# A planner's ranks, its DMA costs and a branch hint in a fused attention, experts and FFN kernel

## The chip, the cores and the metric

The kernel runs on one core of a Trainium2 chip. The metric is device time in microseconds, the median of repeated runs; lower is better. The engines are TensorE (PE, with its weight loads shown apart as PEld), VectorE (DVE), ScalarE (ACT), GpSimd (POOL) and SyncE (SP), which here only issues DMAs. Each engine takes its instructions strictly in the order in which they were written, and the engines wait for one another by semaphores.

## The reference

Three layers follow one another on 2 x 768 tokens: an attention in which a query sees only the keys of its own cluster, a layer of 8 experts of which each token takes one, and an FFN.

```python
# attention: q, k, v are [2, 8, 768, 64], 16 centroids for each head
q_assign = argmax(normed(q) @ normed(c).T)          # k_assign in the same way
scores = where(q_assign == k_assign, q @ k.T / 8, -1e9)
x = softmax(scores) @ v                             # -> [1536, 512]
# experts: w1 [8, 512, 1024], w2 [8, 1024, 512]
logits = x @ w_gate + modality_bias[modality_id]
e = argmax(logits);  p = softmax(logits)[e]
x = p * (relu(x @ w1[e]) @ w2[e])
# FFN: w_in [512, 2048], w_out [2048, 512], alpha [2048]
h = x @ w_in
out = (max(h, 0) + alpha * min(h, 0)) @ w_out
```

The weights of the FFN reach the kernel as 64-bit words. Most products are made from a high and a low part of each operand, in three matmuls.

## The kernel before

**Staging.** The attention runs over 8 groups, each one batch and two heads; a group has 12 units, each 128 queries of one head against all 768 keys. `group_prep` (line 710) prepares a group: it loads k, q and v (line 725), turns k and q on TensorE, finds clusters, moves halves of tiles between partitions (`move`), writes cluster masks (`mask_k`, `mask_q`) and makes fp16 parts of v (`v_abs` on ScalarE, line 916; `v_hi`; `v_lo` on VectorE, line 940). There is one buffer for raw v. `unit` (line 960) makes scores (line 973), the row maximum on VectorE (line 980), the exp on ScalarE (line 992), high and low fp16 parts, a DMA transpose of these (line 1026) into one of four buffers `pt`, and the product with v (line 1034). `group_out` stores the group's rows, and after a batch's last group `route` and `inverse` (lines 1140 and 1102) run chains of small VectorE operations that sort the tokens by expert, and matmuls of line 1134 that invert the order. `slot` (line 1338) is one tile of 128 tokens at one expert; there are 13. The first three use the weights as they are and fill gaps in the attention; the others split weights in two parts (ScalarE, then VectorE) and run after it, in buffers that the attention has left. Tiles that overflow the 13 slots are worked off in a branch (line 1685), which is skipped with these inputs. Ahead of it every engine reads three counts (line 1684).

**FFN.** Behind the branch, `ffn_weight` (line 1493) turns the 64-bit weights into fp32 parts in three VectorE steps (`wb1` to `wb3`, lines 1514 to 1519), then `wf_hi` and `wf_lo`; `gather` (line 1469) fetches the experts' rows in token order into `yg`, scales them (`gated`) and turns them; `ffn` (line 1526) runs, for each batch and each of 16 blocks of hidden columns, 24 first matmuls (line 1544), `neg` and `act` on VectorE (lines 1552 and 1555), `g_hi` on ScalarE, `g_lo` on POOL, and 18 second matmuls (line 1572) into six accumulators. Of eight banks of PSUM, two are left for the first matmuls; four buffers hold activations.

**What sets the order.** Nothing is issued as the code is written: each piece of work is an `Op` with a tag, its possible engines with a planned cost, and a rank `prio`. `Sched.run` (from line 207) plans them one by one on a simulated clock. On each engine, of the operations that could start within a margin `win` of the earliest, the one of lowest rank is taken; the engine for an operation is the one with the earliest planned end plus a `bias`. `ORDER` adds an offset to the rank of each kind (tag). For DMAs the planner keeps `dma_free`, the time up to which transfers are planned. A load of q, k, v or expert weights is kept back while much is planned:

```python
                if o.dma is not None and o.dma[1] == "load":
                    at = max(at, dma_free - self.back)
...
                xfer, kind, busy = o.dma[:3]
                way = "transpose" if kind == "transpose" else e
                dma_free = max(st + self.ISSUE[way], dma_free) + xfer
                o.end = dma_free + 0.13
                free[e] = st + 1.05 if e == "POOL" else max(st + busy, o.end - self.LEAD[way])
```

Then each engine's instructions are written in the planned order. All up to the branch is one plan; the FFN is another, with the same margins and an empty table of offsets (`TAIL`).

## Time and profile before

| | us |
|---|---|
| median of 3 runs | 755.58 (755.41 to 755.67) |
| the profiled execution | 757.23 |
| its span, first to last instruction | 755.4 |
| mean granted TensorE clock, 1 is full | 0.97 |
| TensorE busy | 689.2 |
| VectorE / ScalarE / POOL busy | 512.8 / 410.1 / 306.7 |

A profile is one execution. Times in its views count from the span's start. "Idle before" in a timeline stands in brackets, with what ended it; `ACTq` or `SPq` is an engine's own instruction queue (waits, branches, DMA issues), in which time is not counted as busy. The granted clock is the TensorE clock that the chip allowed, as a share of full speed. The DMA share is the mean busy share of the 16 DMA engines as the records give it, and can pass 1 a little.

### The profile page before, as it was taken

What the parts mean: (1) busy time and instruction counts of PE and PEld (TensorE: products, weight loads), DVE (VectorE), ACT (ScalarE), POOL (GpSimd) and SP (SyncE); (2) the same over time, 40 slices, a digit from 0 to 9 for tenths busy, and PEclk for the clock granted to TensorE, in tenths of its full rate; (3) what the DMA queues carried; (4) which work ended last, traced back from release to release, by engine and by line L of the source; (5) the groups of instructions that cost most, each with busy time, mean ns of one, the idle gap of its engine ahead of it and who ended that gap; (6) DMA issues with size and microseconds to landing.
All of it is one profiled execution on the core that took longest, in us unless ns stands there. A gap on an engine that the chain in (4) does not pass through costs nothing. (4 is left out here: it accounts for less than half of the span.)

```text
span 755.4 us, 13680 instructions
## 1 busy us (share of the span) xinstructions
PE 689.2 (91%) x5041; PEld 581.3 (77%) x5041; DVE 512.8 (68%) x913; ACT 410.1 (54%) x624; POOL 306.7 (41%) x276
## 2 busy tenths in 40 slices
PE   8878899786998779999898897899999999999997
PEld 7767787785777655568686786799999979999996
DVE  6798888889899741799897694587777533322331
ACT  5778988787889642388776894122222341111112
POOL 4467765573667432012232100365555622222221
PEclk9999999997999989999999899799999999999999
DMA  8498899799999989913755610234433030000002
GB/s 202 127 166 186 142 212 220 131 196 234 222 191 184 174 228 171 364 62 103 267 188 184 206 56 32 85 112 127 152 112 112 28 112 1 1 0 1 1 1 84
DMA packets 167418, 101.58 MB, mean 134 GB/s; under 512 B 133136, under 2 KB 147984, under 8 KB 167344
## 3 DMA queue, kind: packets, MB, share of 16 engines
q1 hardware_dynamic: 165136, 93.63, 51.1%
q0 software_dynamic: 2208, 7.00, 3.6%
q8 instruction: 42, 0.69, 0.4%
q14 instruction: 32, 0.26, 0.1%
HBM read 87.37 MB, written 12.85 MB: 133 GB/s over the span
## 5 line engine op out<-in xcount | busy, mean ns | idle before, releaser
L1572 PE MATMUL ps<-wf,ghl 128*128 128x512 f32 x576 | 140.1, 395 | 2.4 <-POOL ghl L420 1.5
L1572 PEld LDWEIGHTS ps<-wf,ghl 128*128 128x128 f32 x576 | 107.8, 189 | 25.2 <-POOL ghl L420 3.1
L1552 DVE TENSOR_SCALAR m<-ps,alp 128x384 f32<-128x384 f32 x64 | 39.5, 617 | 126.3 <-PE ps L1544 126.3
L392 ACT ACTIVATE ghl<-g 128x384 fp32r<-128x384 f32 x64 | 33.7, 526 | 166.7 <-DVE g L1555 166.7
L420 POOL TENSOR_TENSOR p<-p,p 128x768 f16<-128x768 f32 x57 | 95.7, 1682 | 46.1 <-ACT p L392 42.1
L420 POOL TENSOR_TENSOR ghl<-g,ghl 128x384 fp32r<-128x384 f32 x63 | 67.7, 1075 | 113.9 <-ACT ghl L392 113.9
L420 DVE TENSOR_TENSOR whl<-wst,whl 128x1024 fp32r<-128x1024 f32 x80 | 96.8, 1251 | 12.9 <-ACT whl L392 12.9
L980 DVE TENSOR_REDUCE nm<-pss 128x1 f32<-128x768 f32 x96 | 91.0, 950 | 12.3 <-PE pss L973 10.9
L992 ACT ACTIVATE p<-pss,nm 128x768 f32<-128x768 f32 x96 | 86.1, 899 | 22.1 <-DVE nm L986 7.0
L392 ACT ACTIVATE whl<-wst 128x1024 fp32r<-128x1024 f32 x80 | 82.3, 1057 | 11.3 <-PE ps L1458 6.9
L1034 PEld LDWEIGHTS <-pt 128*128 128x128 f16 x1152 | 60.9, 99 | 21.7 <-DMA pt<-p 12.9
L1034 PE MATMUL ps<-v,pt 128*128 128x65 f16 x1152 | 68.9, 196 | 9.2 <-DMA pt<-p 8.1
L1544 PE MATMUL ps<-x2a,wf 128*128 128x384 f32 x384 | 73.0, 347 | 4.0 <-ACTq L1685 4.0
L1544 PEld LDWEIGHTS ps<-x2a,wf 128*128 128x128 f32 x384 | 70.4, 195 | 5.7 <-ACTq L1685 4.4
L973 PE MATMUL pss<-s1k,s1q 128*128 128x384 f32 x192 | 60.1, 395 | 16.1 <-ACT p L992 15.4
L1544 PE MATMUL ps<-x2b,wf 128*128 128x384 f32 x384 | 69.8, 338 | 0.0
L1544 PEld LDWEIGHTS ps<-x2b,wf 128*128 128x128 f32 x384 | 67.7, 188 | 1.2
L1458 PE MATMUL ps<-whl,hTs 128*128 128x512 f32 x240 | 63.1, 401 | 2.0 <-DVE hTs L420 1.2
L1428 PE MATMUL ps<-whl,xTs 128*128 128x512 f32 x240 | 63.9, 407 | 1.0 <-ACT xTs L392 1.0
L420 POOL TENSOR_TENSOR wf<-tw,wf 128x1024 fp32r<-128x1024 f32 x16 | 40.5, 2532 | 55.8 <-ACT wf L392 55.8
L1458 PEld LDWEIGHTS ps<-whl,hTs 128*128 128x128 f32 x240 | 44.5, 190 | 13.1 <-DVE hTs L420 2.4
L1428 PEld LDWEIGHTS ps<-whl,xTs 128*128 128x128 f32 x240 | 45.3, 193 | 11.3 <-ACT xTs L392 1.4
(246 smaller groups left out, 1182.8 us busy)
## 6 DMA issues: line engine op xcount, KB each, us to landing
wst<-in_moe_w_dram SPq DMA_DIRECT2D x104, 512.0 KB
wst<-in_moe_w_in_dram SPq DMA_DIRECT2D x8, 1024.0 KB
wst<-in_moe_w_out_dram SPq DMA_DIRECT2D x8, 1024.0 KB
ys_d<-ys SPq DMA_DIRECT2D x13, 256.0 KB
raw<-in_k_dram SPq DMA_DIRECT2D x8, 384.0 KB
raw<-in_q_dram SPq DMA_DIRECT2D x8, 384.0 KB
vraw<-in_v_dram SPq DMA_DIRECT2D x8, 384.0 KB
x_d<-xg SPq DMA_DIRECT2D x8, 384.0 KB
```

The costliest lines, as they stand in the source:

```text
L392: nc.scalar.activation(out=out, in_=in_, func=AF.Copy)
L420: ENG[e].tensor_tensor(out=out, in0=a, in1=b, op=ALU.subtract)
L973: nc.tensor.matmul(s.t[:, jj, 0:HS], hd["12"[i], "q"].t[:, h, j, qs], hd["12"[i], "k"].t[:, h, jj], start=(i == 0), stop=(i == 1))
L980: S.op({"DVE": c_dve(SEQ)}, lambda e: nc.vector.tensor_reduce(out=nm.t, in_=s.t[:, :, 0:HS], axis=AX.XY, op=ALU.max, negate=True), r=[s], ...
L992: S.op({"ACT": c_act(SEQ) + 0.04}, lambda e: nc.scalar.activation(out=p.t, in_=s.t[:, :, 0:HS], func=AF.Exp, bias=nm.t), r=[s, nm], w=[p], ...
L1034: nc.tensor.matmul(o[:, c], pv, vv[:, D:VW], start=(i == 0), stop=(i == 2 * C - 1))
L1428: nc.tensor.matmul(hps[jj].t, lhs(xT, a, ci), rhs(ch, w_, cols), start=(ci == 0 and i == 0), stop=(ci == 3 and i == len(parts) - 1))
L1458: nc.tensor.matmul(yp.t, lhs(hT, a, f), rhs(4 + f // 2, w_, slice((f % 2) * 512, (f % 2 + 1) * 512)), start=(f == 0 and i == 0), stop=(f = ...
L1544: nc.tensor.matmul(hp.t[:, 0:HS], wi[:, a, kk, fs], x2b.t[:, bb, kk, sl], start=(n == 0), stop=(n == 3 * KD - 1))
L1552: S.op({"DVE": c_dve(HS) + 0.055}, lambda e: nc.vector.tensor_scalar(out=m.t, in0=hp.t[:, 0:HS], scalar1=0.0, scalar2=alp.t[:, f:f + 1], o ...
L1572: nc.tensor.matmul(view(), gh.t[:, a, tt * P:(tt + 1) * P], wo[:, bb, f % 2, :], start=(f == 0 and a == 0 and bb == 0), stop=(f == NF - 1 ...
```

## The change

No operation on data is added or taken away. The plan's inputs change, in six ways. `ORDER` has other offsets, for 43 kinds. `PULL` is new: a bias for an engine and a kind. The planned DMA costs change from a transfer time, an issue time and a lead to two times for each DMA (from issue to landing when the queue is empty, and from the landing before it) and a time for which a transpose holds the queue; `back` goes from 2.13 to 2.8, and only three expert slots (`FRESH`) are planned as loading new weights. Some planned costs and margins change. For the FFN, `TAIL` has offsets for five kinds, and there are margins and a `back` of its own. And the branch gets a label and a hint, marked ahead of all planned work, for PE, ACT and SP, that it is likely taken (which here is the jump past the overflow work).

```diff
-ORDER = {"chain_a": 5, "chain_g": 4, "chain_i": -20, "chain_r": -16, "chain_s": -43, "chain_v": -0.5, "consts3": 64,
-         "gate_exp": 29, "idle": 52, "logits": -46, "low": -0.5, "mm": 0.12, "mm2": 0.217, "move": 4, "nat_lo": 0.5,
-         "norm_ln": 71, "p_hi": -0.939, "pos_max": -17, "ptr": 1.658, "qk_hi": -0.534, "relu": 3, "row_max": 0.759,
-         "scaled": 1, "shift": -27, "sims_max": -45, "sm": 84, "smm": 2, "smtr": 1.5, "square_sum": 6, "tr": 78,
-         "tr_gather": 22, "v_hi": 1, "v_scale": -1, "w_lo": -0.161, "wb1": 0.5, "wb3": -7.5, "wf_lo": 46,
-         "xt_out": 3.5, "ys_out": 100, "ys_store": 56}
-
-TAIL = {}
+ORDER = {"avm": -1, "chain_h": 10, "chain_i": 8, "chain_r": -40, "chain_v": 2.02, "evac_hi": -83, "exp": 1,
+         "gated": -13, "late_consts6": 33, "lm": 8, "logits": -112, "mask_q": 56, "mm2": 0.079, "move": 14,
+         "norm_ln": 11, "onehot": -72, "otr": 1, "p_lo": -3.5, "place": 31, "ptr": 3.804, "qk_hi": 11, "relu": -19,
+         "row_max": 0.687, "scaled": -1, "shift": -35, "sims_eq": 1, "sims_max": 1, "sims_out": -31, "sm": 21,
+         "smm": 4, "smtr": -9, "square": 55, "tr": 18, "tr_gather": 93, "v_abs": 61, "v_hi": -48, "v_lo": -6,
+         "v_scale": -1.5, "v_turn": 1, "w_hi": -20, "wb2": 31, "wb3": 109, "ys_store": 37}
+
+PULL = {("gated", "POOL"): 2.1, ("qk_hi", "DVE"): 1.1, ("wf_hi", "ACT"): -2, ("ys_out", "ACT"): -1.1,
+        ("ys_out", "DVE"): -1}
+
+TAIL = {"mm_second": 69, "neg": 40, "tr_gather": 55, "wf_load": 72, "x2_hi": 103}
...
     LANDED = 0.05
-    ISSUE = {"transpose": 2.37, "SP": 1.86, "POOL": 1.9}
-    LEAD = {"transpose": 2.91, "SP": 5.8}
+    CHANGE = 0.3
+    HELD = {True: 1.1, False: 1.6, "load": 1.5, "store": 0.75, "transpose": 0.7}
...
         o.fn = fn
-        o.prio = (self.prio if prio is None else prio) + self.order.get(tag, 0.0)
+        o.prio = self.prio if prio is None else prio
+        o.prio += self.order.get(tag, 0.0)
         o.tag = tag
+        o.bias = {e: (self.bias if bias is None else bias).get(e, 0.0) + PULL.get((tag, e), 0.0) for e in o.eng}
         o.two = tag in TWO
...
         o.dma = dma
-        o.bias = self.bias if bias is None else bias
         o.adds = ()
...
         free = {}
-        dma_free = pool_till = dve_till = t0
+        dma_free = held = pool_dma = pool_till = dve_till = t0
+        last_kind = None
         ready = [o for o in ops if o.ndep == 0]
...
                     continue
-                if o.dma is not None and o.dma[1] == "load":
+                if o.dma is not None and o.dma[2] == "load":
                     at = max(at, dma_free - self.back)
...
                     if e == "DVE" and o.two:
-                        st = max(st, pool_till - 0.1)
-                    if e == "POOL" and not (o.dma and e in (o.dma[3:] or (e,))):
+                        st = max(st, pool_till + 0.01)
+                    if e == "POOL" and not (o.dma and e in (o.dma[4:] or (e,))):
                         st = max(st, dve_till)
+                        if o.tag == "move":
+                            st = max(st, pool_dma + 0.1, pool_till + 0.1)
                     cost = st + c + o.bias.get(e, 0.0)
...
             o.on = e
-            moved = o.dma is not None and e in (o.dma[3:] or (e,))
+            moved = o.dma is not None and e in (o.dma[4:] or (e,))
             if moved:
-                xfer, kind, busy = o.dma[:3]
-                way = "transpose" if kind == "transpose" else e
-                dma_free = max(st + self.ISSUE[way], dma_free) + xfer
-                o.end = dma_free + 0.13
-                free[e] = st + 1.05 if e == "POOL" else max(st + busy, o.end - self.LEAD[way])
+                first, later, kind, busy = o.dma[:4]
+                if kind == "transpose":
+                    done = max(st + busy, held)
+                    free[e] = done + 0.1
+                    first += done - st + (0.0 if last_kind == kind else self.CHANGE)
+                else:
+                    free[e] = st + busy
+                dma_free = max(st + first, dma_free + later)
+                o.end = dma_free
+                held = dma_free - self.HELD[kind]
+                last_kind = kind
+                if e == "POOL":
+                    pool_dma = dma_free
             else:
...
                     pool_till = free[e]
+                    if o.tag == "move":
+                        free[e] += 0.12
             ready.remove(o)
...
     BIG = float(2.0 ** 60)
-    N = dict(s1q=2, s1k=2, s2q=2, s2k=2, p=3, p16=5, pt=4, v16=2, wf_early=2, xs=2, whl=3, whl2=3, whi='A', wlo='D', lead=1, tw=1, wdma=1.0, pss=2, ps1=4, sq=1, bd=1.5, bp=0, ulead=4, pa=2, pb=0, nat=3, hi='*', lo='DP', lo0='PPT', vraw=1, mvp=1, mvb=0, epi=1, rM=2, lob=0.5, idle=40, pace=57, mve='PA', wd=0.3, wa=0.04, wp=0.03, wpl=0.03, wsp=0.07, cs=1, back=2.13, nld=8, lump='cs', mp=90, mps=8, mpn=0, trp=0.5, evp=3, xTs2=0, xtp=9, fl=6, rsh=1, rp0=0, go=-4, so=0, pre=0, fws=5, gs=4, eb=0.8)
+    N = dict(s1q=2, s1k=2, s2q=2, s2k=2, p=3, p16=5, pt=4, v16=2, wf_early=2, xs=2, whl=3, whl2=3, whi='A', wlo='D', lead=1, tw=1, pss=2, ps1=4, sq=1, bd=1.5, bp=0, ulead=4, pa=2, pb=0, nat=3, hi='*', lo='DP', lo0='PPT', vraw=1, mvp=1, mvb=0, epi=1, rM=2, lob=0.5, idle=40, pace=57, mve='PA', wd=0.3, wa=0.06, wp=0.03, wpl=0.04, wsp=0.04, cs=1, back=2.8, nld=8, lump='cs', mp=90, mps=8, mpn=0, trp=0.5, evp=3, xTs2=0, xtp=9, fl=6, rsh=1, rp0=0, go=-4, so=0, pre=0, fws=5, gs=4, eb=0.8)
+    FRESH = ((0, 2), (1, 1), (1, 5))
     W_EARLY = N["wf_early"]
...
                 t.t.rearrange("p h c d -> p h (c d)"),
-                src[b, hs].rearrange("h (p c) d -> p h (c d)", c=C)), w=[t], dma=(0.51, "load", 0.4),
+                src[b, hs].rearrange("h (p c) d -> p h (c d)", c=C)), w=[t], dma=(3.35, 1.5, "load", 0.55),
                 prio=S.prio + (6 if nm == "v" else 0), tag="load_qkv")
...
             n = G * HS
-            ways = {"SP": 0.65, "POOL": c_pts(n), "DVE": c_dve(n, True), "ACT": c_act(n)}
+            ways = {"SP": 0.65, "POOL": c_pts(n), "DVE": c_dve(n, True), "ACT": c_act(n) + 0.2}
             S.op({x: c for x, c in ways.items() if x[0] in N["mve"] + "S"}, fn,
-                 r=[(src, x) for x in K(sp_, sy)] + (zeros if z else []), w=[(dst, x) for x in K(part, y)], dma=(1.42, True, 0.6, "SP"), bias=mv_bias, tag="move")
+                 r=[(src, x) for x in K(sp_, sy)] + (zeros if z else []), w=[(dst, x) for x in K(part, y)], dma=(2.85, 0.95, True, 0.65, "SP"), bias=mv_bias, tag="move")
...
             S.op({"SP": 0.06}, lambda e: nc.sync.dma_start_transpose(out=p16t(pt), in_=p16.t.rearrange("p a s -> p (a s)")),
-                 r=[(p16, 0), (p16, 1)], w=[pt], dma=(1.91, "transpose", 1.43), tag="turn")
+                 r=[(p16, 0), (p16, 1)], w=[pt], dma=(2.7, 1.2, "transpose", 1.43), tag="turn")
         a = accumulator()
...
             S.op({"SP": 0.6 if c0 == 0 else 0.06}, load, r=[(ei, b), (fl, b)], w=[(wst, c0 + x) for x in range(nl)],
-                 dma=((3.44 if always else N["wdma"]) * nl / 2, "load", 0.38), prio=p0 - 5,
+                 dma=(*((3.75, 1.6) if always or (b, j) in FRESH else (0.0, 0.0)), "load", 0.39), prio=p0 - 5,
                  deps=[] if pace is None else [units[pace + c0]], tag="w_load")
...
             in_offset=bass.IndirectOffsetOnAxis(ap=inv.t[:, b, j:j + 1], axis=0)),
-            r=[(inv, b), *xd[0:b + 1]], w=[xs], dma=(0.9, False, 0), prio=p0 - 5, tag="rows_in")
+            r=[(inv, b), *xd[0:b + 1]], w=[xs], dma=(4.6, 1.2, False, 1.05), prio=p0 - 5, tag="rows_in")
         tp = S.new(ps_1)
...
         gather(t, x2[0], posc, NU + 4 + pslot * (MAIN[0] + N["gs"]) + t, own)
+    tc.mark_branch_hint_location("over", "LikelyTaken", [mybir.EngineType.PE, mybir.EngineType.Activation, mybir.EngineType.SP])
     order = S.run()
...
     S.order = TAIL
+    S.back = 12.4
+    S.win = {"DVE": 0.08, "ACT": 0.9, "PE": 0, "POOL": 0.44, "SP": 99}
...
     nb = [nc.values_load(nsl2.t[0:1, b:b + 1], min_val=0, max_val=SLOTS[1]) for b in range(B + 1)]
-    with tc.If(nb[B] > 0):
+    with tc.If(nb[B] > 0, label="over"):
         for b in range(B):
```

The DMA costs left out here change in the same way in every other call that issues a DMA.

## Rows read from the trace of the kernel before

**Rows 1.** Page of the profile, section 1: busy us (share of the span) xinstructions.

```profile
PE 689.2 (91%) x5041; PEld 581.3 (77%) x5041; DVE 512.8 (68%) x913; ACT 410.1 (54%) x624; POOL 306.7 (41%) x276
```

**Rows 2.** Busy time by stage: stretch (us), length, then busy us (xinstructions) of each engine, granted TensorE clock (1.00 is full), DMA share, GB/s.

```profile
160.00:265.00 105.00, 87.75 (x1004) 73.86 (x1000) 91.73 (x193) 84.40 (x128) 60.56 (x51) 0.92 1.11 203
265.00:282.00 17.00, 12.81 (x100) 8.49 (x100) 9.18 (x19) 7.91 (x12) 5.56 (x6) 0.80 0.79 230
282.00:302.00 20.00, 18.64 (x196) 10.33 (x193) 1.95 (x6) 4.81 (x7) 4.84 (x3) 1.00 1.03 172
302.00:468.00 166.00, 156.75 (x728) 118.33 (x726) 138.54 (x210) 121.55 (x162) 29.14 (x19) 0.98 0.46 165
468.00:488.00 20.00, 14.07 (x47) 11.78 (x48) 7.59 (x9) 3.24 (x5) 7.43 (x6) 0.74 0.31 95
...
595.00:626.00 31.00, 29.15 (x149) 24.57 (x148) 10.30 (x17) 11.44 (x20) 11.64 (x12) 1.00 0.26 85
```

**Rows 3.** Instructions of line 1685, the branch: duration ns min/median/max, first and last start us.

```profile
L1685 DVEq COMPARE_BRANCH  x1: 72/72/72, 465.2 to 465.2; - x1
L1685 DVEq EVENT_SEMAPHORE  x1: 21/21/21, 465.5 to 465.5; - x1
L1685 PEldq COMPARE_BRANCH  x1: 3619/3619/3619, 466.0 to 466.0; - x1
L1685 SPq COMPARE_BRANCH  x1: 58/58/58, 468.9 to 468.9; - x1
L1685 ACTq COMPARE_BRANCH  x1: 50/50/50, 469.1 to 469.1; - x1
...
L1685 ACTq EVENT_SEMAPHORE  x1: 17/17/17, 471.8 to 471.8; - x1
```

**Rows 4.** Timeline of TensorE, 440 to 510 us: start us, length us, line, idle before it, releaser.

```profile
462.84 5.05 PE L1458 MATMUL ps<-whl,hTs 128*128 128x512 f32 x21
471.87 6.89 PE L1544 MATMUL ps<-x2a,wf 128*128 128x384 f32 x24 [3.98 <-ACTq L1685]
...
479.76 1.89 PE L1572 MATMUL ps<-wf,ghl 128*128 128x512 f32 x7 [0.49 <-POOL ghl L420]
482.56 0.73 PE L1572 MATMUL ps<-wf,ghl 128*128 128x512 f32 x2 [0.92 <-ACT ghl L392]
...
499.83 4.39 PE L1544 MATMUL ps<-x2a,wf 128*128 128x384 f32 x24
```

**Rows 5.** Busy time in two stretches of 2 us at the branch (columns as in Rows 2).

```profile
470.00:472.00 2.00, 0.14 (x1) 0.14 (x1) 0.00 (x0) 0.00 (x0) 0.00 (x0) 0.60 0.10 30
472.00:474.00 2.00, 2.00 (x7) 2.00 (x8) 0.00 (x0) 0.00 (x0) 0.56 (x1) 0.50 0.03 8
```

**Rows 6.** Timeline of VectorE, 470 to 484 us.

```profile
478.88 1.90 DVE L1517 SCALAR_TENSOR_TENSOR tw<-wst,tw 128x1024 int32<-128x1024 int32 x1
480.71 0.60 DVE L1552 TENSOR_SCALAR m<-ps,alp 128x384 f32<-128x384 f32 x1
```

**Rows 7.** Timeline of SyncE's DMA queue, 222 to 302 us.

```profile
244.89 19.93 SPq L1026 DMA_TRANSPOSE pt<-p  x9
...
267.44 1.21 SPq L725 DMA_DIRECT2D vraw<-in_v_dram  x1
...
280.98 15.46 SPq L1026 DMA_TRANSPOSE pt<-p  x8
```

**Rows 8.** Timeline of VectorE, 216 to 221 us.

```profile
218.06 1.15 DVE L940 SCALAR_TENSOR_TENSOR v<-vraw,vsc,v 128x384 f16<-128x384 f32 x2 [0.68 <-ACT v L394]
```

**Rows 9.** Busy time of 2 us in the tail of the attention (columns as in Rows 2).

```profile
277.00:279.00 2.00, 2.00 (x7) 1.35 (x6) 1.15 (x2) 1.58 (x3) 0.84 (x1) 0.50 0.05 17
```

**Rows 10.** Timeline of TensorE around the routing of batch 0.

```profile
179.20 0.19 PE L1134 MATMUL ps<-T,M 128*128 128x6 f16 x2 [3.63 <-ACT xg L1057]
```

**Rows 11.** Timeline of TensorE, 244 to 249 us.

```profile
248.01 0.20 PE L1034 MATMUL ps<-v,pt 128*128 128x65 f16 x1 [3.11 <-DMA pt<-p]
```

**Rows 12.** Instructions on the tile yg, the rows gathered for the FFN.

```profile
L401 POOL TENSOR_SCALAR yg<-yg,gate x5: 692/697/1880, 393.5 to 611.3; 128x512 f32<-128x512 f32 x5
```

## The prediction

> **What bounds the kernel now.** I read the page's busy shares first, then the busy time cut by stage, then the places where a stage loses time. TensorE is busy 689.2 of 755.4 us and no other engine passes 513 [rows 1], so at most 66 us can come from its idle time, and something more from stretches in which its clock is low. The stage table [rows 2] shows where. From 160 to 265 us, the attention of batch 1, four things are nearly full at once: the DMA engines (share 1.11), VectorE (91.73 of 105), ScalarE (84.40) and TensorE (87.75, at a granted clock of 0.92); an order that helps one of them alone wins little. From 265 to 282 us TensorE does 12.81 of 17 us at clock 0.80, while VectorE and ScalarE are half idle: nothing is full there but, for most of it, the DMA engines. From 302 to 468 us, the experts, TensorE has 156.75 of 166: little is left. From 468 to 488 us, around the branch, it has 14.07 of 20 at clock 0.74. From 595 to 626 us, where batch 1 enters the FFN, 1.85 of 31 are idle; the rest of the FFN has none but its end. So the places that can pay are the end of the attention and the branch.

> **The branch hint.** The branch of line 1685 is skipped with these inputs. VectorE leaves it at once: its compare takes 72 ns and its next semaphore comes 0.3 us after [rows 3]. TensorE's own compare takes 3619 ns, begun at 466.0 while the last matmuls still run. ScalarE's takes 50 ns at 469.1, but its next instruction comes only at 471.8, and that is what releases TensorE: its last expert matmuls start at 462.84 for 5.05 us, and the first of the FFN starts at 471.87 after 3.98 us of idle time, released by ACTq L1685 [rows 3, 4]. So the wait that ends last is the 2.65 us on ScalarE behind a branch that itself takes 0.05. VectorE shows that such a wait need not be. The three engines that the change hints are the long branch and the two other late ones. If the jump's target is there in time, ScalarE is through at about 469.2, TensorE's own compare is long over, SP's is at 468.9, and the FFN starts 2.6 us earlier. Not removed: the reads of the count ahead of the branch.

> [...]

> Second, the clock. [...] Sum for the hint: 2.6 + 2.5 = 5.1 us.

> **The new plan's DMA costs, and one load.** In the planner a load of q, k, v or expert weights may not start before the DMA time planned so far less `back`. Before, SP is free again 2.78 us ahead of the end of a transpose's transfer (its end is 0.13 later, and 2.91 is taken off), and `back` is 2.13: a load comes 0.65 us after SP is free, so a transpose that is ready in that time goes first, whatever the load's rank. After, SP is free 2.6 us ahead of that end and `back` is 2.8: the load may start as soon as SP is free, and its rank (some 20 ahead of the transposes of its time) puts it first. The trace shows the loss. There is one buffer for raw v. VectorE's last use of it for group 6 starts at 218.06 and lasts 1.15 us [rows 8]; the load of group 7's v is issued at 267.44, after runs of transposes such as nine in 19.93 us [rows 7]: 48 us late. Without v the products of group 7 can't start, their four transposed buffers stay full, and the last eight transposes only start at 280.98; in the stage that holds this, TensorE idles 4.19 us, and at clock 0.80 loses as much as 0.20 x 17 = 3.4 more [rows 2]; the DMA engines, until then full, stand at 0.05 for two us [rows 9]. An early load lets the transposes run on; what is queued behind it on SP waits for its issue, 1.21 us. The gain is bounded from below by the DMA gap, which can be closed even if transposes are the limit (about 2 us), and from above by TensorE's whole loss, 7.6 us. I take 5, nearer the middle: the stage before is full of DMA work, so not all comes through, while what was waited for (12 tiles' products) also ends sooner and lets the experts' second weight buffers open earlier, a stage where VectorE is at 138.54 of 166.

> **The table of 43 kinds.** Most offsets reorder work on engines that are full between 160 and 265 us, where the sum of the work is unchanged; I count that at 0. One can be named. The routing chains of batch 0 had ranks -43 and -20 ahead of the row maxima and now have 0 and +8, behind them. Now TensorE stops there once for 3.63 us [rows 10]. In the whole stage the clock can cost as much as 0.08 x 105 = 8.4 us [rows 2]; I allow this stop a third, 2.8. So the bounds are 0 and about 6.5 us, and I take 0, because the DMA engines (1.11) set the end of that stage. The bias against gating on POOL moves up to five scalings of 0.697 us [rows 12] to engines that were not full in the FFN: 0. The other offsets have no row of their own; I bound them by one border between groups that stalls, 6 us (below), and the same gained. The plan's other new costs (transfers, reciprocals, moves on ScalarE, three expert slots marked as loading anew) change no instruction, only the order, and are in the same bound.

> **The FFN.** Ranking the second matmuls 69 back changes little: only two accumulator banks and four activation buffers let the first ones run ahead. It lets batch 1 start ahead of batch 0's last second matmuls; at most the 1.85 us of idle time at 595 to 626 [rows 2]. Against it, `neg` 40 back puts the weight steps ahead of it on VectorE. Now one such step of 1.90 us starts just before it and delays it to 480.71, and TensorE waits 0.49 and 0.92 us for what follows [rows 4, 6]. One more step ahead costs 1 to 2 us at the start; later two spare banks hide it. I take 0, bounds 2 us slower and 2 faster. The margins of 0.9 on ScalarE and 0.44 on POOL choose among waiting evictions of 31 us where these engines are a third busy [rows 2]: 0. SyncE's margin of 99 there puts output stores ahead of weight loads; the longer `back` of 12.4 touches no load of the FFN, as these aren't marked as held back: 0.

> **The sum.** 2.6 + 2.5 + 5 + 0 + 0 = 10.1 us. The profiled execution took 757.23 us with a span of 755.4; the median of the runs is 755.58. Taken off the execution this is 747.1, off the median 745.5, and I predict the median: 745.5.

> **Rivals.**
> - The hint does nothing, because the target is not held over 466 us: 755.6 - 5 = 750.6. [...] Against it: VectorE shows that a jump at this place can be through in 0.3 us; no row shows how long a hint holds, so its chance is a judgment.
> - The load comes early but the DMA engines set the end anyway, or other orders take the gain back: 755.6 - 5.1 = 750.5. For it: the share of 1.11.
> - More comes through: the routing stop goes too, 745.5 - 6.5 = 739.0. Against it: the same share.
> - Slower. The abs of v on ScalarE is now ranked 61 back. Without it the next group's products can't start, and ScalarE runs 84.40 of 105 us, so it may wait through a group's worth of exps, as it now waits for its load. A border that stalls like the one measured costs between 4.19 and 7.6 us, say 6, and a smaller one is in the trace already: 3.11 us of waiting for a transpose [rows 11]. The load's gain then goes as well. With one border the change breaks even, 755.6 - 5.1 + 6 = 756.5; from two on it is slower, 762.5. Against it: in each group ScalarE has a fifth of its time free, and a step of rank 61 back takes the first gap.

> **How the numbers follow.** Chances: forecast 0.45, hint without effect 0.13, load without gain 0.15, more 0.08, slower 0.19. A measurement can tell about 0.2%, 1.5 us. Of the two middle rivals about half a tenth ends within that of 755.6: same 0.07, faster 0.74, slower 0.19. The range reaches from the sum with all upper bounds but the FFN's (7.6 for 5, 6.5 for 0: 736) to a little past one stalled border, 758; only the cases beyond either end are left out.

> **What the changed profile would show.** Hint: the compare on TensorE well under 1 us, ScalarE's next instruction within 0.3 us of its compare, TensorE idle about 1.3 us before the FFN, the first 24 matmuls in about 4.4 us. Load: the eighth v load issued within some us of the last use of the buffer, no gap in the transposes before the last group's end, and the FFN's start earlier by about 5 us plus the hint's share. Wrong would be: ScalarE idle in front of the abs of v at several borders, or a longer stretch from 160 to 302 us; or TensorE idle after 488 us, which would put the fault into the FFN.

## The result and the profile after

The changed kernel takes **741.94 us** (median; 741.18 to 743.36) against 755.5 us for the kernel before: ratio 0.982 [0.981, 0.984], 13.6 us faster. 745.5 was predicted, in a range of 736 to 758. The profiled execution took 741.18 us, its span is 739.2 where that of before is 755.4. All line numbers are some 18 to 21 higher than before (the branch is line 1706).

The page of after, section 1, busy us and share of the span, answers to [rows 1]: TensorE is busy 10.5 us less for the same 5041 instructions, which is clock (0.986 on the mean instead of 0.97; in the three other runs of the changed kernel it is 0.974 to 0.980), and idle 60.5 instead of 66.2 us, 5.7 less.

```profile
PE 678.7 (92%) x5041; PEld 574.3 (78%) x5041; DVE 511.6 (69%) x916; ACT 410.1 (55%) x630; POOL 310.8 (42%) x274
```

Busy time by stage of after, with the columns of [rows 2]:

```profile
160.00:265.00 105.00, 87.35 (x986) 72.85 (x985) 85.79 (x187) 81.21 (x122) 60.88 (x58) 0.94 1.09 210
265.00:282.00 17.00, 12.94 (x178) 10.57 (x174) 11.46 (x19) 10.90 (x14) 6.56 (x5) 1.00 1.03 197
282.00:302.00 20.00, 18.27 (x174) 10.97 (x171) 4.87 (x11) 8.58 (x14) 6.19 (x4) 1.00 0.83 186
...
319.00:456.00 137.00, 133.96 (x645) 105.64 (x643) 126.61 (x143) 115.61 (x153) 30.05 (x16) 1.00 0.43 147
456.00:476.00 20.00, 17.52 (x82) 16.06 (x83) 11.02 (x14) 4.53 (x8) 8.40 (x7) 0.91 0.31 94
482.00:580.00 98.00, 95.08 (x473) 84.57 (x472) 71.46 (x82) 23.51 (x34) 55.82 (x35) 1.00 0.33 110
580.00:611.00 31.00, 30.64 (x157) 26.35 (x156) 10.15 (x17) 12.38 (x22) 10.10 (x9) 1.00 0.26 85
```

and the stage of before that answers to 319 to 456 us:

```profile
319.00:468.00 149.00, 139.75 (x654) 109.08 (x652) 127.00 (x147) 117.63 (x155) 28.14 (x18) 0.98 0.41 143
```

I split both spans at two points: the first split of an expert's weights on ScalarE (tile whl), and the end of the last expert matmul. Before: 319.3, then 148.6, then 287.5 us. After: 319.1, 136.4 and 283.8. So the attention, for which half of the gain was predicted, gave nothing; **12.2 of the 16.2 us come from the experts' stage**, of which the prediction said that little is left; and 3.7 lie from the branch on, of which up to 1.7 is a second stretch at half clock, from 484.1 to 487.5 us, that the trace of before alone shows there. Of the 12 us between the two stage rows, 6.2 are idle time of TensorE (9.25 to 3.04) and 5.8 busy time: 3.4 of these are clock, as will be seen, the rest some work that now lies ahead of the stage (x654 to x645).

The branch, as in [rows 3]: instructions of line 1706, duration in ns and start, and ahead of them the hint, which the trace has under line 1769 at 0.8 us (TensorE's at 0.9), some 450 us before the branch.

```profile
L1769 ACTq BRANCH_PREFETCH_HINT  x1: 45/45/45, 0.8 to 0.8; - x1
...
L1706 PEldq COMPARE_BRANCH  x1: 481/481/481, 453.8 to 453.8; - x1
...
L1706 ACTq COMPARE_BRANCH  x1: 68/68/68, 456.8 to 456.8; - x1
L1706 ACTq EVENT_SEMAPHORE  x1: 17/17/17, 457.2 to 457.2; - x1
```

TensorE's timeline of after around it, and further on in the FFN (start, length, idle before and its releaser), as in [rows 4]:

```profile
457.30 6.00 PE L1562 MATMUL ps<-x2a,wf 128*128 128x384 f32 x24 [1.84 <-ACTq L1706]
464.12 0.74 PE L1590 MATMUL ps<-wf,ghl 128*128 128x512 f32 x2 [0.82 <-ACT ghl L410]
...
495.62 4.49 PE L1562 MATMUL ps<-x2a,wf 128*128 128x384 f32 x24 [1.03 <-DVE g L1573]
```

ScalarE is through 0.4 us after its compare instead of 2.65, TensorE's compare takes 0.48 instead of 3.62 us, and the idle time is 1.84 instead of 3.98. But 24 matmuls still take 6.00 us and not 4.39. SyncE's queue, as in [rows 7]: the load of the last group's v is issued at 226.75, 40.7 us earlier, and the attention ends no sooner for it.

```profile
226.75 0.40 SPq L743 DMA_DIRECT2D vraw<-in_v_dram  x1
...
236.31 25.49 SPq L1044 DMA_TRANSPOSE pt<-p  x11
```

What the experts' stage lost before is a stop that stands in no row of the prediction. Three timelines of the kernel before, of POOL, ScalarE and TensorE:

```profile
408.72 0.96 POOL L1474 DMA_INDIRECT yg<-ys_d,posc  x1 [0.30 <-issue]
```
```profile
415.38 0.72 ACT L394 ACTIVATE yg<-yg,gate 128x512 f32<-128x512 f32 x1 [5.00 <-DMA yg<-ys_d,posc]
416.00 0.58 ACT L1437 ACTIVATE hb<-ps 128x512 f32<-128x512 f32 x1
```
```profile
416.63 1.12 PE L1451 MATMUL ps<-ident,hb 128*128 128x128 f32 x4 [4.23 <-ACT hb L1437]
```

POOL issues a gather of expert outputs for the FFN at 408.72. ScalarE stands in front of the scaling of these rows from 410.4 to 415.38, 6.7 us after the gather's issue; behind it in the same queue is the relu of the next expert (hb), and behind that TensorE. The planner before put the gather's landing at 1.9 + 0.9 + 0.13 = 2.93 us after its issue, the changed one at 3.9, where no other transfer is planned ahead of it. Behind the stop the clock is low too: from 415 to 422 us before, and in the same stretch after (columns of [rows 2]):

```profile
415.00:422.00 7.00, 5.37 (x15) 4.40 (x16) 4.18 (x4) 5.50 (x8) 0.00 (x0) 0.56 0.80 286
```
```profile
415.00:422.00 7.00, 7.00 (x34) 5.78 (x33) 4.92 (x6) 5.27 (x7) 0.00 (x0) 1.00 0.85 294
```

### The profile page after: what moved, and what is told of

It reads as the page before. It is cut to its first block, busy times and chain, and to the rows that moved or that the text cites. A ratio compares the mean times of both kernels' runs of the same rounds, so it can differ in the third digit from the quotient of the medians.

```text
span 739.2 us, 13709 instructions
## 1 busy us (share of the span) xinstructions
PE 678.7 (92%) x5041; PEld 574.3 (78%) x5041; DVE 511.6 (69%) x916; ACT 410.1 (55%) x630; POOL 310.8 (42%) x274
## 5 line engine op out<-in xcount | busy, mean ns | idle before, releaser
L1590 PE MATMUL ps<-wf,ghl 128*128 128x512 f32 x576 | 137.7, 392 | 1.5 <-ACT ghl L410 0.8
L1590 PEld LDWEIGHTS ps<-wf,ghl 128*128 128x128 f32 x576 | 107.1, 188 | 23.5 <-POOL ghl L438 1.6
L438 POOL TENSOR_TENSOR ghl<-g,ghl 128x384 fp32r<-128x384 f32 x62 | 70.6, 1142 | 122.0 <-ACT ghl L410 116.7
L438 DVE TENSOR_TENSOR whl<-wst,whl 128x1024 fp32r<-128x1024 f32 x80 | 93.7, 1215 | 3.5 <-ACT whl L410 3.4
L1052 PEld LDWEIGHTS <-pt 128*128 128x128 f16 x1152 | 60.5, 99 | 37.0 <-DMA pt<-p 31.2
L1562 PEld LDWEIGHTS ps<-x2a,wf 128*128 128x128 f32 x384 | 68.6, 192 | 8.4 <-DVE g L1573 4.9
L1573 DVE SCALAR_TENSOR_TENSOR g<-ps,m 128x384 f32<-128x384 f32 x64 | 35.6, 556 | 52.6 <-POOL ghl L438 50.4
```

The costliest lines, as they stand in the source:

```text
L438: ENG[e].tensor_tensor(out=out, in0=a, in1=b, op=ALU.subtract)
L1052: nc.tensor.matmul(o[:, c], pv, vv[:, D:VW], start=(i == 0), stop=(i == 2 * C - 1))
L1562: nc.tensor.matmul(hp.t[:, 0:HS], wi[:, a, kk, fs], x2b.t[:, bb, kk, sl], start=(n == 0), stop=(n == 3 * KD - 1))
L1573: S.op({"DVE": c_dve(HS)}, lambda e: nc.vector.scalar_tensor_tensor(out=g.t, in0=hp.t[:, 0:HS], scalar=0.0, in1=m.t, op0=ALU.max, op1=ALU. ...
L1590: nc.tensor.matmul(view(), gh.t[:, a, tt * P:(tt + 1) * P], wo[:, bb, f % 2, :], start=(f == 0 and a == 0 and bb == 0), stop=(f == NF - 1 ...
```

## The experiments

All in one table; the three columns in the middle are the stretches defined above, read from each kernel's trace. On the chips of these runs the kernel before spreads from 748 to 760 us, so times are compared as ratios to it, and the stretches tell where. Executions of one order differ too. Before, hint_only, gather_late and hint_gather run the same instructions in the same order up to the first split and reach it at 313.1 to 319.3 us (mean 315.3); the five kernels with the changed order (changed, run again, after_no_hint, after_old_ffn, after_gather) reach it at 317.9 to 320.1 (mean 319.0). So the new order of the attention gains nothing and may cost some 4 us.

| kernel | to the first split | experts | branch to end | median us | ratio to before |
|---|---|---|---|---|---|
| before | 319.3 | 148.6 | 287.5 | 755.5 | 1 |
| changed | 319.1 | 136.4 | 283.8 | 741.94 | 0.982 [0.981, 0.984] |
| changed, run again | 317.9 | 135.6 | 284.4 | 742.69 | 0.986 [0.982, 0.990] |
| hint_only | 314.0 | 148.9 | 282.5 | 749.80 | 0.994 [0.992, 0.997] |
| after_no_hint | 319.9 | 135.6 | 287.1 | 742.57 | 0.984 [0.979, 0.988] |
| gather_late | 313.1 | 141.0 | 284.3 | 743.61 | 0.988 [0.983, 0.993] |
| v_load_early | 326.5 | 132.6 | 286.6 | 747.75 | 0.992 [0.988, 0.995] |
| hint_gather | 314.6 | 140.8 | 281.2 | 739.72 | 0.982 [0.977, 0.986] |
| three | 325.5 | 135.2 | 280.4 | 745.21 | 0.988 [0.984, 0.992] |
| plan_only | 332.2 | 137.9 | 284.2 | 757.18 | 1.003 [1.000, 1.007] |
| order_only | 346.4 | 147.5 | 283.9 | 777.75 | 1.027 [1.022, 1.033] |
| routing | 335.4 | 134.1 | 285.7 | 757.81 | 1.003 [0.999, 1.007] |
| after_old_ffn | 320.1 | 135.5 | 281.8 | 737.43 | 0.977 [0.972, 0.981] |
| after_gather | 318.0 | 141.6 | 285.9 | 746.47 | 0.989 [0.985, 0.994] |

**The hint alone**, in the kernel before.

```diff
+    tc.mark_branch_hint_location("over", "LikelyTaken", [mybir.EngineType.PE, mybir.EngineType.Activation, mybir.EngineType.SP])
     order = S.run()
-    with tc.If(nb[B] > 0):
+    with tc.If(nb[B] > 0, label="over"):
```

> The kernel before, with the branch label and the hint and nothing else. If the hint acts by itself: TensorE's compare falls from 3.62 us to under 1, ScalarE's next instruction comes 0.3 to 0.5 us behind its compare instead of 2.65, and the FFN starts about 2.1 to 2.6 us earlier: 753.0 of 755.5. If the clock then stays up, as the prediction had it, 2.5 us more: 750.4; in the changed kernel the first 24 matmuls took 6.00 us, so I now expect only part of that. Rival: what shortened the idle time in the changed kernel is its new order ahead of the branch, and the hint does nothing: 755.5.

It gives 4.2 us [2.1, 6.3]. TensorE in the trace of hint_only:

```profile
464.70 6.00 PE L1544 MATMUL ps<-x2a,wf 128*128 128x384 f32 x24 [1.80 <-ACTq L1686]
```

The idle time falls by 2.2 us. The clock still falls behind it, for 3.4 us instead of 6.8: in the matmuls the gain is 0.9, not 2.5.

**The changed kernel without the hint**, the two lines above taken out.

> The changed kernel without the label and the hint. If the hint acts: idle time ahead of the FFN goes back to about 4 us, and the time is 2.1 to 4.5 us above the changed kernel's 741.9, so 744.0 to 746.5. Rival: no change, 741.9.

The idle time of 3.99 us is back in front of the FFN, and the last stretch is 287.1 us against 283.8 and 284.4: 3 us in the trace. The times don't resolve it: 742.57 us lies below the 744.0 to 746.5 expected.

**The gather planned later**, in the kernel before, so that its landing is planned 5.0 us behind its issue; nothing else (`dma_free` moves with it, and so do the transfers planned behind a gather).

```diff
-   ... w=[yg], dma=(0.9, False, 0), tag="rows")
+   ... w=[yg], dma=(3.0, False, 0), tag="rows")
```

> The kernel before, with one planned cost changed: the gather of the experts' rows is planned to land 5.0 us after its issue instead of 2.9 (its transfer is planned as 3.0 instead of 0.9). The order up to about 388 us stays as it was. Theory from the two traces: most of the gain lies in the experts' stage, and there in waits like the one of 4.23 us before 416.63, where ScalarE's scaling of a gathered row sat for 5.00 us in ScalarE's queue, planned too early, and held up the relu behind it; a later planned landing takes that wait and the low clock behind it (3.4 us of work) away: 748 to 750. Rival: the stage won by the table's offsets for the experts' evictions, and this cost alone gives nothing: 755.5.

9.1 us [5.7, 12.6] faster. The instructions keep their order up to 388 us, so what lies ahead of that (313.1 instead of 319.3) is the spread between executions, which hint_only shows with 314.0 as well. The experts' stretch is 141.0 against 148.6 and 148.9 with the stop: 7.6 to 7.9 us, as expected of a stop of 4.2 us and 6.8 us at half clock (4.2 + 3.4). In the trace of **hint_gather**, hint and gather together, ScalarE no longer scales these rows here, and the clock stays up. The wait itself is not gone. The gather issued at 402.76 is waited for until 411.30, longer than before, but by POOL, and neither ScalarE nor TensorE stands behind it:

```profile
402.76 1.97 POOL L1474 DMA_INDIRECT yg<-ys_d,posc  x1 [0.30 <-ACT x2a L392]
...
411.30 1.17 POOL L401 TENSOR_SCALAR yg<-yg,gate 128x512 f32<-128x512 f32 x1 [5.69 <-DMA yg<-ys_d,posc]
```
```profile
415.00:422.00 7.00, 7.00 (x34) 5.77 (x34) 7.00 (x8) 6.40 (x10) 1.52 (x2) 1.00 0.86 328
```

> The kernel before with the hint and the later planned gather landing, nothing else. If the two gains are of different places, they add: 0.9944 and 0.9879 of before give 0.9823, the same as the whole change. Rival: the later gather's 9 us held some of the hint's (both runs had shorter low clock at the FFN's start), and the pair gives about 0.986.

These three lines of code give 0.982 [0.977, 0.986], as much as the whole change on the same chip, 0.986 [0.982, 0.990]:

> The changed kernel itself, to stand beside the next three on the same chip. Every theory: its ratio to the kernel before as measured first, 0.982 (0.979 to 0.986).

**The early load of v**, in the kernel before: the load of the last group alone is not held back.

```diff
-   ... w=[t], dma=(0.51, "load", 0.4),
+   ... w=[t], dma=(0.51, True if nm == "v" and (b, g) == (1, 3) else "load", 0.4),
```

> The kernel before, with one load changed: that of v for the last group is no longer held back by the planned DMA time. By the prediction's term this closes the gap in the transposes and is worth 5 us (2 to 7.6): 750.5. Rival, from the changed kernel, whose eighth v load came at 226.8 instead of 267.4 while the last product with v ended at 299.8 instead of 300.6: the DMA engines set the end of that stage, so the end moves by under 1 us and the time stays at 755.5 (754.5 to 756.5).

It is 6.3 us faster, but by neither theory. The last product with v ends at 289.2 us, against 294.5 to 300.7 in the four traces with the order of before, so the DMA engines alone don't set that end. Yet the first split is later (326.5), and the time is won in the experts' stretch, where the order has shifted and the stop at the gather is gone. So it was put on top of hint_gather as well, where that stop can't be won again:

> The same pair, and the last group's v load not held back. If the load's 6.3 us were its own (the end of the attention came 6 to 11 us earlier), they add to the pair: 0.974. Rival: in the run of the load alone the stop at 416 us was gone too, only because everything behind had shifted, and first-weights slots finished later; then the load itself is worth about nothing, and the time is the pair's, 0.980 to 0.986.

There it **costs** 5.5 us (745.21 to 739.72; the intervals of the ratios, [0.984, 0.992] and [0.977, 0.986], just overlap). The tail of the attention in the trace of three:

```profile
265.00:282.00 17.00, 12.18 (x187) 10.94 (x188) 8.81 (x15) 10.67 (x15) 7.95 (x5) 0.84 1.13 211
282.00:302.00 20.00, 16.05 (x116) 10.35 (x113) 5.89 (x31) 1.58 (x3) 0.00 (x0) 0.71 0.86 257
```

The load is issued at 218.98 and the last product of the attention ends at 288 instead of 296 us; but TensorE's stretch at half clock lies behind the hole, across 276 to 293 us, and the experts start 11 us later. What fills the tail is gone. SyncE's queue in the kernel before, then in three, and TensorE in three:

```profile
268.87 5.10 SPq L1358 DMA_DIRECT2D wst<-in_moe_w_dram  x8
```
```profile
266.66 18.02 SPq L1026 DMA_TRANSPOSE pt<-p  x9
284.89 1.91 SPq L1358 DMA_DIRECT2D wst<-in_moe_w_dram  x3
```
```profile
290.15 2.07 PE L1458 MATMUL ps<-wst,hT 128*128 128x512 f32 x2 [2.02 <-DMA wst<-in_moe_w_dram]
```

The hole between the transposes was of use. In the kernel before, eight weight loads of the first three slots go out in it, and 48 of the 96 matmuls of these slots (the products that read wst) run ahead of the last product with v, between the transposes. With the early load the transposes run on, the weight loads come behind them, TensorE waits for a weight, and 20 of 96 run ahead; the other 28 (ten of them take 4.46 us there) are some 12 us of work that now stands in front of the experts. A part of the loss may also be a stop of 1.70 us at 415.15, behind ScalarE's scaling of a gather, which is back in three.

**The new costs without the new ranks**: the changed kernel with the old table, no pulls, no hint, the FFN as before.

> The changed kernel's planned DMA costs, margins, back and marked slots, with the ranks of before, no engine bias, no hint and the FFN's plan as before. If the planned landings are what pays: the experts' stage has no stop behind a gather, and the ratio is 0.984 to 0.990. Rival: the new costs need the new ranks, and with the old ones the time is that of before or above: 0.998 to 1.01.

**The new ranks and pulls without the new costs**, in the kernel before.

> The kernel before with the changed kernel's ranks of kinds and its engine pulls alone: old transfer costs, old margins, no hint. Theory A (the stop behind the gather goes because the new costs plan the gather's landing later; ranks alone leave the landing planned 2.9 us after its issue): PE still stops for 1 to 5 us behind a scaling that waits for the gather, or the ranks, found for other costs, fit badly and the first slot products come later; 752 to 770 us. Theory B (the ranks alone reorder ScalarE's queue so that the stop goes): the experts' stage loses less than 4 us beside its work and the time is 742 to 748 us. The stop at the branch (3.6 to 4.0 us) stays in either.

Neither half is faster: 1.003, the rival's number, and 1.027, past the range of theory A. The new costs remove TensorE's stop: ScalarE's scaling at 404.36 has no wait ahead of it, later ones wait 1.73 us on ScalarE and 6.05 on POOL, and the waits that are left to TensorE from 319 to 470 us in plan_only are two, 0.9 and 0.8 us. But with the old ranks they leave a hole at the end of the attention:

```profile
282.00:302.00 20.00, 11.21 (x175) 9.35 (x171) 6.08 (x13) 4.39 (x5) 6.51 (x5) 0.67 1.02 193
```

Where the changed kernel has 18.27 us at clock 1.00 in this stretch, this one has 11.21 at 0.67, and its first split comes 13 us later. With the new ranks alone TensorE idles 9.1 us in the experts' stage, as much as before (4.10 of it for VectorE, 1.80 behind ScalarE's scaling of a gather), and 27 us are lost ahead of it. So what the ranks contribute is to fill the tail that the new costs would empty. The count of the first slots' matmuls says the same: ahead of the last product with v run 28 of 96 in plan_only and 50 of 96 in the changed kernel, where SyncE sends weight loads singly between the transposes:

```profile
285.55 0.11 SPq L1376 DMA_DIRECT2D wst<-in_moe_w_dram  x1
285.84 1.46 SPq L1044 DMA_TRANSPOSE pt<-p  x1
```

Which of the 43 kinds do that stays open.

**Two ranks of the routing chains alone**, in the kernel before.

```diff
-ORDER = {... "chain_i": -20, ... "chain_s": -43, ...}
+ORDER = {... "chain_i": 8, ...}
```

> The kernel before with two ranks of the routing chains changed alone (the kind at -43 back to none, the one at -20 to 8, as in the changed kernel). Theory A (the stop of PE at the routing is not set by these ranks alone, and what is gained there is waited for later): within 2.5 us of before, 753 to 758 us. Rival B (the stop shrinks and all later work moves up with it): 3 to 6.5 us faster. Rival C (the order after it shifts, so that the stop behind the gather of the experts' stage goes as it did with the early load): 6 to 9 us faster with the stop at the routing unchanged.

757.81 us, no gain, as theory A had it. TensorE's stop at the routing stays, now in front of another product:

```profile
PE ps L748 <- ACT xg L1057: 3.4, 1, 3.4
```

Again two effects cancel: the first split at 335.4, 16 us late (20 of the 96 matmuls run ahead of the last product with v), and an experts' stretch in which TensorE has no idle time to speak of:

```profile
335.00:469.00 134.00, 133.96 (x643) 107.00 (x642) 116.10 (x117) 115.03 (x149) 25.03 (x20) 1.00 0.44 150
```

**The changed kernel with the old FFN**: none of the five kinds moved, the margins as they stood.

```diff
-TAIL = {"mm_second": 69, "neg": 40, "tr_gather": 55, "wf_load": 72, "x2_hi": 103}
+TAIL = {}
-    S.back = 12.4
-    S.win = {"DVE": 0.08, "ACT": 0.9, "PE": 0, "POOL": 0.44, "SP": 99}
+    S.win["ACT"], S.win["POOL"], S.win["SP"] = 0.04, 0.03, 0.07
```

> The changed kernel without the FFN's part: no kinds moved there, and the margins of choice in the FFN as they stood. Theory A (the FFN's part is worth nothing: PE is the bound there): within 2 us of the changed kernel, ratio to before 0.980 to 0.987. Rival B (the FFN's part costs, by the pauses of 1.0 us that PE has there behind VectorE's products): 2 to 4 us faster than the changed kernel. Rival C (it gains): 2 to 4 us slower, ratio above 0.987.

This is the fastest of all, 737.43 us, ratio 0.977 [0.972, 0.981]. From the branch on it takes 281.8 against 283.8 and 284.4 us: the FFN's part of the change costs 2 to 3 us in the traces (by the ratios 4 to 7 us, to the two medians of the changed kernel; one of their two intervals overlaps with this one). Why, is to be seen where the changed kernel stops at 495.62. VectorE there:

```profile
490.43 1.49 DVE L1532 TENSOR_SCALAR tw<-wst 128x1024 int32<-128x1024 int32 x1 [3.60 <-POOL wf L438]
...
493.22 1.23 DVE L1537 SCALAR_TENSOR_TENSOR tw<-wst,tw 128x1024 int32<-128x1024 int32 x1
...
495.00 0.56 DVE L1573 SCALAR_TENSOR_TENSOR g<-ps,m 128x384 f32<-128x384 f32 x1
```

and TensorE at the same place in after_old_ffn:

```profile
490.13 4.37 PE L1562 MATMUL ps<-x2a,wf 128*128 128x384 f32 x24
494.34 3.58 PE L1590 MATMUL ps<-wf,ghl 128*128 128x512 f32 x15
```

In both kernels three weight steps keep VectorE from the accumulators until 494. With the old ranks TensorE has second matmuls (L1590) left for that time; with these ranked back it has done them before, and waits for a bank. Three such stops are 2.8 us. A second cost lies at the FFN's start. In the changed kernel ScalarE stands there in front of a scaling again, 6.79 us, with `ghl` behind it, for which TensorE waits; in after_old_ffn `ghl` goes first, at 462.44. ScalarE in the changed kernel:

```profile
462.94 0.72 ACT L412 ACTIVATE yg<-yg,gate 128x512 f32<-128x512 f32 x1 [6.79 <-DMA yg<-ys_d,posu]
463.57 0.51 ACT L410 ACTIVATE ghl<-g 128x384 fp32r<-128x384 f32 x1
```

The run takes out all of the FFN's part at once, so its five ranks and its margins are not told apart.

**The changed kernel with the gather planned at 6.0 us** instead of 3.9.

```diff
-   ... w=[yg], dma=(3.9, 0.9, False, 1.05), tag="rows")
+   ... w=[yg], dma=(6.0, 0.9, False, 1.05), tag="rows")
```

> The changed kernel with the gather of the expert outputs planned to land 6.0 us after its issue instead of 3.9. Theory A (in the changed kernel no engine stands behind a gather any more, so the gain of that plan is already in it): within 2.5 us of the changed kernel, 740 to 745 us. Rival B (3.9 us is still too early for gathers that land 5 to 6.6 us after their issue, so that some of the remaining idle time of PE goes): 736 to 740 us. Rival C (a later landing moves the scalings behind the FFN's start or delays the last stores): 745 to 750 us.

It is slower than the changed kernel, 746.47 us, within rival C's numbers but by a cause that I hadn't named: the stop comes back on another queue. POOL, VectorE and TensorE:

```profile
385.67 6.57 POOL L1492 DMA_INDIRECT yg<-ys_d,posc  x1 [0.30 <-issue]
```
```profile
394.72 1.47 DVE L417 TENSOR_SCALAR yg<-yg,gate 128x512 f32<-128x512 f32 x1 [2.91 <-DMA yg<-ys_d,posc]
...
396.71 0.68 DVE L438 TENSOR_TENSOR hTs<-ps,hTs 128x512 fp32r<-128x512 f32 x1
```
```profile
397.44 0.80 PE L1476 MATMUL ps<-whl,hTs 128*128 128x512 f32 x1 [2.85 <-DVE hTs L438]
```
```profile
397.00:404.00 7.00, 6.56 (x20) 5.48 (x21) 6.74 (x8) 2.92 (x5) 0.98 (x2) 0.52 0.60 190
```

Here a gather occupies POOL for 6.57 us and lands 9 us after its start; the scaling stands in VectorE's queue for it, the eviction hTs behind the scaling, and TensorE behind that, for 2.85 us with 6.8 at half clock after it: 2.85 + 3.4 = 6.3, and the experts' stretch is 5.2 to 6.0 us longer than in the two runs of the changed kernel.

## Why the prediction was right, and where it wasn't

The time is 3.6 us below the forecast, and the sign is right. The sum is right for a part only.

- **The branch wait, 2.6 us: right.** It is 2.1 to 2.2 us in the traces with the hint, and ScalarE is through 0.4 us after its compare, nearly as VectorE without a hint. The hint stands ahead of the whole scheduled stream, some 450 us before the branch, and it holds: the compare on TensorE takes 0.48 us instead of 3.62. The rival that it would not hold falls.
- **The clock behind it, 2.5 us: mis-sized.** In the sum this term has the first 24 matmuls at full clock, in 4.39 us instead of 6.89 [rows 4, 5], behind 1.3 us of idle time; no run shows a gain of 2.5. The idle time was 1.84 us, the clock was at half for 3.4 us behind it, and the 24 matmuls take 6.00 us: 0.9. The hint is thus worth 3 us in the changed kernel's trace, and 4.2 by the times of hint_only, not 5.1. Nor would full clock have brought the rest in the changed kernel. When it was run again, the clock stayed up behind the same 1.84 us, and the second matmuls started 6.8 us after the first ones all the same, because they waited for `ghl`:

```profile
455.37 4.45 PE L1562 MATMUL ps<-x2a,wf 128*128 128x384 f32 x24 [1.84 <-ACTq L1706]
462.18 0.73 PE L1590 MATMUL ps<-wf,ghl 128*128 128x512 f32 x2 [2.36 <-ACT ghl L410]
```

- **The load of v, 5 us: wrong.** The load came 40.7 us earlier, as derived, and the attention ended 0.8 us earlier (299.8 instead of 300.6). TensorE's idle time from 160 to 302 us went from 22.8 to 23.4 us; only its owner changed. The heads of the two lists of TensorE's waits (total us, times, longest), of before and of after, show to whom:

```profile
PE pss L973 <- ACT p L992: 7.4, 10, 1.8
PE ps L1034 <- DMA pt<-p: 4.3, 4, 3.1
PE ps L1134 <- ACT xg L1057: 3.6, 1, 3.6
```
```profile
PE ps L1052 <- DMA pt<-p: 15.3, 13, 2.9
PE pss L991 <- ACT p L1010: 5.4, 6, 2.0
```

  The failing step is "bounded from below by the DMA gap" and, behind it, the step from products that end sooner to "the experts' second weight buffers open earlier". In v_load_early and three the last product with v does end sooner, at 289 and 288 us instead of 294.5 to 300.7, and the experts start 11 to 12 us later than in hint_gather: eight weight loads of the first slots had gone out in that gap. On top of hint_gather the load is a loss of 5.5 us. The rival that the load would bring nothing, at 0.15, has the right number for this part, but not the reason: the DMA engines alone don't set that end, for in the kernel before the early load moves it. What keeps it at 298.6 to 300.8 us in the five traces of the changed order stays open, and what it would cost to hold the load back there was not tried.
- **The table, 0 us: not shown as a term of its own.** The routing's stop of 3.63 us [rows 10] is gone from the list of after, though not by the two ranks that the prediction named, with which it stays at 3.4 (routing); and what it gave is waited for at the transposes. The table isn't idle: without it the new costs give 1.003, with it and the FFN's part and the hint 0.98; without the new costs it gives 1.027.
- **The experts' stage: missed.** "156.75 of 166: little is left" took nine idle microseconds in a stage as spread over many small waits. One row holds 4.23 of them, with 3.4 more by the clock behind it, and the diff changed the very cost that had planned it: the prediction read "the plan's other new costs" as one lump within ±6 us. Planning that landing later is worth 9.1 us by itself (gather_late, where 748 to 750 was expected and 743.6 measured); in the changed kernel the stage loses 9.6 us less (6.2 idle, 3.4 clock).
- **The FFN, 0 with 2 either way: mis-sized.** It costs 2 to 3 us. "Ranking the second matmuls 69 back changes little" is the step that failed, as the traces read: they are what TensorE does while VectorE is busy with weight steps. The margins on ScalarE and POOL, put at 0 as well, were taken out in the same run; the scaling ahead of `ghl` may be theirs.

In stretches, the 16.2 us of the two spans are 0.2 to the first split, 12.2 in the experts' stage and 3.7 from the branch on, the last being a hint of 3 to 5 less an FFN's part of 2 to 3 and the spread between executions. The forecast came near by luck: a gain of 5 that didn't exist stood in for one of 10 that the sum had at 0.

## What to carry to other kernels

Before calling a stage nearly full, list its longest single waits: one stop of 4 us behind a transfer, in a queue that the bound engine depends on, cost its length (4.23 us) and the low clock after it (6.8 us at half, 3.4 of work) here, and taking it away was worth more than the new table by itself. Where an order is planned ahead, compare the planned landing of each kind of transfer with the trace, and see what stands behind its consumer in the queue; planning it later by a fixed amount can still move the stop elsewhere, and here it helped by moving the wait to an engine that nobody stood behind. Before closing a hole in one queue, see what else uses it. New costs and new ranks are one thing: either half alone was no faster here, so neither can be priced by itself.
